# One weight quarter's load, issued on ScalarE's queue instead of SyncE's: a mixed linear and local attention block

## The chip, the cores and the metric

The kernel runs on one core of a Trainium2 chip. The metric is device time in microseconds (us): the median of several executions. All times inside an execution are counted from its first instruction, as the profile counts them.

## The reference

Two attention blocks of 2,048 tokens and width 1,024 read the same `x`. One is linear attention, the other local and dilated. A sigmoid gate mixes their outputs.

```python
x = A_x
g = _sigmoid((x * gate_w).sum(-1, keepdims=True))
a = _A_ref(x, A_wqkv, A_wo)      # linear attention: phi(q), phi(k), kv = sum of phi(k) v^T
b = _B_ref(x, B_wqkv, B_wo)      # 8 keys at distance 2, softmax
return g * a + (1 - g) * b
```

Only the first step matters here: `phi(k)` of block A, the projection `x @ wqkv[:, D:2D]`.

## The kernel before

The first thing that TensorE computes is the projection of the first four row blocks of `x` (128 rows each) on the key weights `WkA`. The weights come in two column halves of 512 columns, and each half in four k quarters of 256 rows (256 KB). The transposed `x` (called `xT`) comes in k quarters too: the first is loaded as plain rows and transposed on TensorE, the others by a transposing DMA.

```python
def load_rows(eng, t0, t1, d0=0, d1=D): ...     # x's rows, plain                     (L89)
def load_xT(k, t0, t1): ...                     # nc.sync.dma_start_transpose          (L95)
def load_wk(eng, k, h): ...                     # k quarter k of column half h, 256 KB (L99)
# ... (the identity for the transposes is made on VectorE)
with tc.manual_schedule(engines={SP, mybir.EngineType.Activation}):
    for kt in range(2):
        nc.scalar.dma_start(out=WkA[0][:, kt, :], in_=A_wqkv[kt * P:(kt + 1) * P, D:D + 512])
    load_rows(nc.sync, 0, 2, 0, 2 * P)
    load_rows(nc.sync, 2, 4, 0, 2 * P)
    load_wk(nc.sync, 0, 1)        # "the quarter": the one that the change moves
    load_xT(1, 0, 4)              # "xT's second quarter"
    load_wk(nc.sync, 1, 0)        # "the second load"
    load_wk(nc.sync, 1, 1)
    # ... k quarters 2 and 3, then everything else
```

TensorE works in program order:

```python
warm_up(26)                       # 26 small matmuls on ones
transpose_rows(0)                 # needs rows 0 and 1
for t in range(2): project(first[t], t, 0, 0)
transpose_rows(2)                 # needs rows 2 and 3
for t in range(2): project(first[t], t, 1, 0)
for half, ts in ((0, (2, 3)), (1, range(4))):   # half 1 needs the quarter: 9th projection matmul
    for kt in range(2):
        for t in ts: project(first[4 * half + t], t, kt, half)
for k in range(1, 4):             # k = 1 needs xT's second quarter and the second load: 17th
    for half in range(2):
        for t in range(4):
            for kt in (2 * k, 2 * k + 1): project(first[4 * half + t], t, kt, half)
    # ... phi on ScalarE and VectorE
```

Three landmarks are used below. **T** is the start of TensorE's first transpose (it needs rows 0 and 1). **H** is the start of the 9th projection matmul (it needs the quarter). **K** is the start of the 17th (it needs xT's second quarter and the second load).

The softmax here doesn't subtract the row's maximum and nothing guards it: scores larger than these inputs give would overflow.

## Time and profile before

| | before |
|---|---|
| time, three runs at first | 472.21 us median (472.11 to 472.75) |
| span of the profiled run | 470.1 us |
| TensorE busy | 466.1 us |
| T, H, K in the first profile | 3.74, 6.67, 8.46 us |
| matmuls from K to the last one of the kernel | last starts at 467.12 us |

TensorE is the bound, so the question is never how busy something else is, but where TensorE stands still. The prediction shows the lines for that. In all lines of the profile, PE is TensorE's matmuls and PEld its weight loads (which run ahead of the matmuls), DVE is VectorE, ACT ScalarE, POOL GpSimd; SPq is SyncE issuing DMAs; L196 is the line of the kernel with the projection matmul, L210 and L211 those of the transposes and their copies, L99 and L95 those of the loads.

### The profile page before, as it was taken

How to read it: one execution, taken by the hardware profiler on the slowest of the kernel's cores; microseconds unless marked ns; L12 is line 12 of the kernel's file. 1: busy time of each engine (PE TensorE's matmuls, PEld its weight loads, DVE VectorE, ACT ScalarE, POOL GpSimd, SP SyncE). 2: the span in 40 equal slices, each digit the busy share in tenths (PEclk: the TensorE clock that was granted, in tenths of full speed). 3: DMA queues.
4: the chain of work that ended last, by engine and by line, in shares of the span. 5: the costliest groups of instructions: out<-in, count | busy, mean ns of one | idle time of the engine just before them, and what ended most of it. 6: DMA issues, size and time to landing. Idle time of an engine off the chain costs nothing.

```text
span 470.1 us, 13202 instructions
## 1 busy us (share of the span) xinstructions
PE 466.1 (99%) x5762; PEld 268.8 (57%) x5762; DVE 278.4 (59%) x612; ACT 169.4 (36%) x277; POOL 15.7 (3%) x30
## 2 busy tenths in 40 slices
PE   8999999999999999999999999999999999999997
PEld 5444444445444444444888888888874444444444
DVE  2586689990219999999666676667660049800000
ACT  1343311112433333334455555555543234221121
POOL 1500000400000000000000000000000000000000
PEclk9999999999999999999999999999999999999999
DMA  9999970000644243627326525442463913211111
GB/s 222 206 218 374 348 244 0 0 1 1 216 134 123 83 141 123 157 97 244 111 55 108 112 52 87 104 93 62 83 172 67 234 57 79 73 52 45 34 33 46
DMA packets 98189, 55.14 MB, mean 117 GB/s; under 512 B 69075, under 2 KB 90579, under 8 KB 98131
## 3 DMA queue, kind: packets, MB, share of 16 engines
q1 hardware_dynamic: 93090, 49.87, 41.0%
q10 hardware_dynamic: 5040, 4.43, 2.9%
q8 instruction: 45, 0.74, 0.7%
q14 instruction: 14, 0.11, 0.1%
HBM read 26.10 MB, written 15.86 MB: 89 GB/s over the span
## 4 chain that ended last, share of the span: by engine, by line
PE 98%; DMA 1%; SPq 0%; DVE 0%; issue 0%; DVEq 0%
PE q_ps L421 26%; PE d_ps L627 12%; PE p_ps L325 12%; PE g_ps L264 12%; PE e_ps L627 12%; PE pk_ps L196 11%; PE p_ps L361 9%; PE po L501 2%; PE s2b L479 2%; DMA WkA<-in_A_wqkv_dram 1%; PE kv_ps L284 0%; PE w_ps L180 0%; SPq L89 0%; DVE osb L634 0%; DVEq L634 0%
## 5 line engine op out<-in xcount | busy, mean ns | idle before, releaser
L421 PE MATMUL q_ps<-xT,WqB 64*64 64x512 bf16 x1024 | 70.3, 376 | 0.0
L421 PE MATMUL q_ps<-xT,WkB 64*64 64x512 bf16 x1024 | 69.8, 376 | 0.0
L171 DVE TENSOR_SCALAR e<-e 128x512 f32<-128x512 f32 x64 | 27.3, 427 | 61.8 <-ACT e L170 61.8
L325 PE MATMUL p_ps<-WvB,xT 128*128 128x512 bf16 x256 | 57.4, 379 | 0.0
L196 PE MATMUL pk_ps<-WkA,xT 128*128 128x512 bf16 x256 | 55.8, 379 | 0.4 <-DVE xT L211 0.3
L264 PE MATMUL g_ps<-pk,xrow 128*128 128x512 bf16 x256 | 55.4, 379 | 0.0
L484 ACT ACTIVATE PT<-s2b 128x928 bf16<-128x928 f32 (+4 forms) x40 | 34.2, 855 | 49.8 <-PE s2b L479 48.8
L486 DVE TENSOR_TENSOR PT<-PT,mask 128x928 bf16<-128x928 bf16 (+4 forms) x40 | 23.6, 590 | 36.3 <-ACT PT L484 36.3
L421 PEld LDWEIGHTS <-WkB 64*64 64x64 bf16 x1024 | 40.4, 107 | 6.9 <-DMA vd<-tmp 0.2
L361 PE MATMUL p_ps<-WqA,xT 128*128 128x512 bf16 x192 | 43.4, 379 | 0.0
L627 PEld LDWEIGHTS <-pqT 128*128 128x128 bf16 x272 | 26.0, 98 | 29.6 <-issue 0.2
L627 PEld LDWEIGHTS <-OBT 128*128 128x128 bf16 x272 | 26.0, 98 | 29.4
L421 PEld LDWEIGHTS <-WqB 64*64 64x64 bf16 x1024 | 39.4, 107 | 5.6 <-DVE qz L461 0.2
L264 PEld LDWEIGHTS <-xrow 128*128 128x128 bf16 x256 | 25.0, 98 | 30.2
L196 PEld LDWEIGHTS <-xT 128*128 128x128 bf16 x256 | 24.8, 98 | 30.7 <-DVE xT L211 0.8
L325 PEld LDWEIGHTS <-xT 128*128 128x128 bf16 x256 | 24.9, 98 | 30.2 <-issue 0.5
L634 DVE TENSOR_SCALAR osb<-e_ps,omg 128x128 bf16<-128x128 f32 x1 | 0.4, 351 | 57.6 <-PE e_ps L627 57.6
L501 PEld LDWEIGHTS <-PT 64*56 64x56 bf16 (+2 forms) x1152 | 29.9, 104 | 4.5
L330 ACT CAST tmp<-p_ps 128x512 bf16<-128x512 f32 x32 | 18.7, 587 | 37.7 <-PE p_ps L325 32.8
L170 ACT ACTIVATE e<-pk_ps 128x512 f32<-128x512 f32 x32 | 18.9, 597 | 36.5 <-PE pk_ps L196 32.8
L361 PEld LDWEIGHTS <-xT 128*128 128x128 bf16 x192 | 18.8, 98 | 22.6
L627 PE MATMUL d_ps<-WoA,pqT 128*128 128x512 bf16 (+1 forms) x136 | 30.9, 370 | 0.0
(71 smaller groups left out, 544.3 us busy)
## 6 DMA issues: line engine op xcount, KB each, us to landing
vd<-tmp SPq DMA_DIRECT2D x16, 264.0 KB
out_dram<-osb ACTq DMA_DIRECT2D x31, 128.0 KB
xrow<-in_A_x_dram SPq DMA_DIRECT2D x3, 1024.0 KB
pqd<-tmp SPq DMA_DIRECT2D x12, 256.0 KB
WvA<-in_A_wqkv_dram SPq DMA_DIRECT2D x2, 1024.0 KB
WoA<-in_A_wo_dram SPq DMA_DIRECT2D x2, 1024.0 KB
WvB<-in_B_wqkv_dram SPq DMA_DIRECT2D x2, 1024.0 KB
WqA<-in_A_wqkv_dram SPq DMA_DIRECT2D x2, 1024.0 KB
```

The lines of the kernel that those rows point to most:

```text
L170: nc.scalar.activation(out=e[:], in_=pj[:], func=ACT.Exp)
L171: nc.vector.tensor_scalar(out=e[:], in0=e[:], scalar1=1.0, scalar2=1e-6, op0=ALU.min, op1=ALU.add)
L196: nc.tensor.matmul(pj[:], lhsT=xT[:, kt, t * P:(t + 1) * P], rhs=WkA[half][:, kt, :], start=(kt == 0), stop=(kt == KT - 1))
L264: nc.tensor.matmul(pj[:], lhsT=xrow[:, t, kt * P:(kt + 1) * P], rhs=pk[:, t, half * 512:(half + 1) * 512], start=(t == 0), stop=(t == NB - 1))
L325: nc.tensor.matmul(st["pj"][:], lhsT=xT[:, kt, t * P:(t + 1) * P], rhs=WvB[half][:, kt, :], start=(kt == 0), stop=(kt == KT - 1))
L330: nc.scalar.copy(out=v[:, half * 16:(half + 1) * 16, 0:Dh], in_=st["pj"][:].rearrange("p (h e) -> p h e", h=16))
L361: nc.tensor.matmul(st["pj"][:], lhsT=xT[:, kt, t * P:(t + 1) * P], rhs=WqA[half][:, kt, :], start=(kt == 0), stop=(kt == KT - 1))
L421: nc.tensor.matmul(banks[o][64 * j:64 * j + 64, :], lhsT=lhsT(r, kt, j), rhs=rhs(r, kt), start=first and kt == 0, stop=kt == KT - 1, skip_ ...
L484: nc.scalar.activation(out=pt[:, :, 0:W_], in_=s2b[:].rearrange("p a b s -> p (a b) s")[:, :, 0:W_], func=ACT.Exp, scale=SCALE)
L486: nc.vector.tensor_tensor(out=pt[:, :, 0:W_], in0=pt[:, :, 0:W_], in1=mask[:, None, base:base + W_].broadcast_to([P, 4, W_]), op=ALU.mult)
L501: nc.tensor.matmul(o2[64 * h:64 * h + w, par, s_, i, :], lhsT=pt[r, i, o:o + w], rhs=V[r, m, 4 * c + i, :], start=True, stop=True)
L627: nc.tensor.matmul(st["ps"][:, 0:n], lhsT=lhsT, rhs=W[c0 // 512][:, c, c0 % 512:c0 % 512 + n], start=(side == 0 and c == 0), stop=(side == ...
```

## The change

The quarter is needed by the 9th projection matmul, and TensorE waited for it. The change issues it on ScalarE's queue, behind the two loads that stand there. SyncE then has one issue less before xT's second quarter and the second load.

```diff
         for kt in range(2):
             nc.scalar.dma_start(out=WkA[0][:, kt, :], in_=A_wqkv[kt * P:(kt + 1) * P, D:D + 512])
+        load_wk(nc.scalar, 0, 1)
         load_rows(nc.sync, 0, 2, 0, 2 * P)
         load_rows(nc.sync, 2, 4, 0, 2 * P)
-        load_wk(nc.sync, 0, 1)
         load_xT(1, 0, 4)
         load_wk(nc.sync, 1, 0)
         load_wk(nc.sync, 1, 1)
```

## The prediction

> **What bounds the kernel now.** I read the page first, then who waited for whom on TensorE's two rows, then the chain that ended last over the first 12 us, then SyncE's issues, the bandwidth by stretch, and at last single instruction starts and the DMAs' semaphore increments in the trace. From the page of the kernel before, busy time and the chain:
>
> ```profile
> span 470.1 us, 13202 instructions
> ...
> PE 466.1 (99%) x5762; PEld 268.8 (57%) x5762; DVE 278.4 (59%) x612; ACT 169.4 (36%) x277; POOL 15.7 (3%) x30
> ...
> PE 98%; DMA 1%; SPq 0%; DVE 0%; issue 0%; DVEq 0%
> ```
>
> TensorE is busy for 466.1 of 470.1 us and is 98% of the chain that ended last. A load can only matter where TensorE waits for it. The view of waits of the weight-load row, from 3 to 12 us:
>
> ```profile
> PEld L196 <- DVE xT L211: 0.8, 2, 0.4
> PEld L196 <- DMA WkA<-in_A_wqkv_dram: 0.6, 1, 0.6
> PEld L210 <- DMA xrow<-in_A_x_dram: 0.2, 1, 0.2
> PEld L196 <- issue: 0.2, 1, 0.2
> ```
>
> The second line is the wait that the change is aimed at: WkA's second column half, first quarter (256 KB), which L120 issues. The 0.6 us is idle time of the weight loads, which run ahead of the matmuls, so it overstates what TensorE lost. The chain in order of time, same stretch:
>
> ```profile
> 1.82 4.79 DMA WkA<-in_A_wqkv_dram
> 6.62 0.05 issue
> 6.67 5.41 PE pk_ps L196 x24
> ```
>
> The DMA was issued at 1.82 and landed at 6.62 (1.82 + 4.79, rounded). From 6.67 the chain shows only projection matmuls. SyncE's issues, by the timeline of its queue, and the stretches (PE, PEld, DVE, ACT, POOL busy, clock, DMA share, GB/s):
>
> ```profile
> 0.80 0.98 SPq L89 DMA_DIRECT2D xrow<-in_A_x_dram  x2
> 1.82 0.47 SPq L99 DMA_DIRECT2D WkA<-in_A_wqkv_dram  x1
> 2.34 1.49 SPq L95 DMA_TRANSPOSE xT<-in_A_x_dram  x1
> 3.88 1.08 SPq L99 DMA_DIRECT2D WkA<-in_A_wqkv_dram  x2
> ```
>
> ```profile
> 4.50:6.75 2.25, 2.13 (x13) 0.84 (x13) 0.29 (x1) 0.41 (x2) 0.00 (x0) 1.00 1.03 163
> 6.75:8.50 1.75, 1.75 (x9) 0.75 (x10) 0.00 (x0) 0.00 (x0) 0.00 (x0) 1.00 1.12 324
> ```
>
> Taking the quarter off SyncE brings every later issue of SyncE forward by one slot, 2.34 - 1.82 = 0.52 us. But the DMA engines are full in both stretches (share 1.03 and 1.12), and in the first, in which the quarter and the transposed load of xT's second quarter are in flight together, they move only half the rate (163 against 324 GB/s).
>
> **How much TensorE really loses.** In the trace single 128x512 matmuls start 0.216 us apart when nothing holds them (6.665, 6.890, 7.106). The last matmul of the first column half's first quarter starts at 6.169, so the next could start at 6.385. It starts at 6.665: 0.28 us lost to the DMA. Eight matmuls follow. The last starts at 8.185 and the next could start at 8.401. It starts at 8.461: 0.06 us lost. From there to 115 us I find no gap of over 0.05 us between matmul starts, so everything behind 8.461 is rigid and moves as one piece.
>
> That second, small gap is the important one. The matmul at 8.461 is the first of the second k quarter, and waits for WkA's first column half, second quarter (issued at 3.88). The 16th and last semaphore increment of that DMA is at 8.42. The x rows for it (xT's second quarter) were there at 7.67. So **two loads stand in a row**: the one aimed at (landed 6.62) and the next one (landed 8.42), and only 0.04 us lie between the second landing and the rigid part. All the gain there can be is the two gaps, 0.28 + 0.06 = 0.34 us, or 0.07% of 472 us, and only if both loads land earlier. If the first alone does, TensorE runs its eight matmuls earlier and waits at the second.
>
> **What the Trainium skill says.** (1) "DMA: Bandwidth & Descriptors", section "Issuing engines are not separate DMA queues": transfers of all issuers run on the same 16 engines and interleave, and issuing from several saves only sequencer time. The trace agrees: ScalarE's two loads (queue q10) and the first rows (q1) are in flight side by side from 2.0 to 4.0 us. (2) Same page, "Queues, rings and completion order": each DMA engine takes turns between the queues that have work, packet by packet. So on ScalarE's queue the quarter no longer goes ahead of xT's transposed load, it shares with it, and it shares with the rows instead of coming behind them. No run shows yet what this sharing costs. (3) Same page, "Why a DMA increments its semaphore by 16 and not by 1": only all 16 mean that the data is there. Here that counts: the quarter's increments begin at 4.99 and four are in by 5.10, yet the other twelve come between 6.48 and 6.62. (4) "TensorE: Matmul & The Clock Gate", section "Wait — 56ns, not 53.3ns?", gives 215.7 ns between warm matmuls of 512 columns. The trace's 0.216 us agrees.
>
> **The change part by part.** Removed: one issue of 0.47 us from SyncE at 1.82. Added: one issue on ScalarE, whose two loads there (411 and 450 ns) end at 1.72; the third then ends near 2.2 (estimate from those), and ScalarE's first own work, the copy at 4.17, is not touched. Moved: the transposed load is issued at 1.82, the second quarter's first half near 3.36. Instructions and bytes are the same: nothing on TensorE, VectorE or in evictions changes, so the sum outside the first 8.5 us is zero.
>
> The quarter itself: 256 packets of 1 KB, 16 on an engine, about 46 ns each undisturbed, so 0.74 us of engine time. Its packets now start behind ScalarE's second load (landed 4.17), and not behind rows 2 to 3 (landed 4.51). On the face of it that is 0.3 us earlier, enough for the first gap of 0.28. But it then alternates with the transposed load, which was behind it in the ring.
>
> The second load: up to its landing the same five pieces have to pass: rows 256 KB, ScalarE's 256 KB, the quarter 256 KB, xT 256 KB, itself 256 KB, together 1,280 KB from 1.75 to 8.42 us, 197 GB/s. Engines that are full do not end sooner for another order of the same packets. Its landing moves only as far as the slow stretch gets shorter, somewhere from 0 to the 0.52 us of the earlier issue. I take some 0.15 us, which leaves 0.15 of the possible 0.34.
>
> **The rivals.** (a) *The whole gain*: if the slow stretch comes from descriptors that SyncE makes late (its transposed issues take 1.28 to 1.90 us each), both loads land up to 0.52 us earlier, and the full 0.34 us comes out: 471.9 us. Against it speaks the DMA share of 1.03 in that stretch. (b) *The next wait takes its place*: the quarter lands early, the second load stays at 8.42, and the matmul at 8.461 does not move: 472.2 us. For it speaks that all bytes ahead are the same. (c) *Contention makes it worse*: rows 2 and 3 landed at 4.51 and are used at 4.635, 0.12 us of slack. With the quarter's 16 packets among them they may be up to 0.74 us later, shifting TensorE by 0.62 us there: 6.385 + 0.62 = 7.0, plus eight matmuls of 0.216 is 8.73, against 8.461 a loss of 0.27 us. Likewise if the mixing slows the quarter to 7.1 us: 7.1 + 1.73 = 8.83, a loss of 0.37. That makes 472.5 to 472.6 us. For it speaks that the mixed stretch is the slow one already. (d) *Something later*: an earlier SyncE queue could upset the loads behind. They have room: xT's fifth row block lands at 14.97 and its first use, 48 matmuls after 8.461, is near 18.8.
>
> **Range and chances.** I hold (a) for a quarter, (b) or between (a) and (b) for a half, (c) for a quarter. 0.25 x -0.34 + 0.5 x -0.1 + 0.25 x 0.3 is about -0.06, and leaning a little to the intent I say -0.1: 472.1 us. The spread of the runs is larger than the effect: three runs before were 472.11, 472.21 and 472.75, and the profiled one 471.84. Low end: 471.84 less 0.34 is 471.5, rounded out to 471.4. High end: 472.75 plus half of the loss of (c) is 472.9. A difference of 2% is 9.4 us, some 28 times all the waiting that the change can reach, so within 2% is all but certain: 0.98, with 0.01 on either side for what I don't see.
>
> **What would show it.** Right: the DMA wait of 0.6 us is shorter or gone; the first matmul of the second k quarter starts between 8.1 and 8.5; the wait in front of it has grown; and TensorE has no new gap behind. Wrong: that matmul starts after 8.5 (contention), with the first rows or the quarter landing late; or before 8.1, which would need a shorter path than TensorE's own; or any change in instruction counts, clock or the stages behind 10 us.

## The result

The changed kernel takes 472.06 us (median of six runs, 471.83 to 472.46), the kernel before 472.16 us in the six runs it was compared with (471.75 to 472.75). The ratio is 0.9998, with a 95% interval from 0.9985 to 1.0011: the same. Ratios here are the mean time of one kernel's runs over that of the other's of the same rounds, so not quite the ratio of the quoted medians.

The page of the changed kernel has the same instructions and the same shape:

```profile
PE 466.2 (99%) x5762; PEld 265.9 (57%) x5762; DVE 278.1 (59%) x612; ACT 169.6 (36%) x277; POOL 15.7 (3%) x30
...
PE 99%; DMA 1%; DVE 0%; issue 0%; DVEq 0%
```

The waits of TensorE's weight loads from 3 to 12 us, all of them (what waited, for what, us in total, times, longest):

```profile
PEld L196 <- DVE xT L211: 0.8, 2, 0.4
PEld L210 <- DMA xrow<-in_A_x_dram: 0.4, 1, 0.4
```

The wait for WkA's load is gone, as intended. The wait for x's first rows is 0.2 us longer. The chain that ended last, in order of time over the first 12 us (start, us, what; pieces left out at the dots):

```profile
0.80 3.01 DMA xrow<-in_A_x_dram
...
4.60 0.60 PE pk_ps L196 x2
5.20 0.22 PE xt_ps L210 x4
5.43 6.71 PE pk_ps L196 x31
```

No load stands in the chain behind x's first rows. SyncE's queue, by the timeline (start, us, engine line, operation):

```profile
1.83 1.34 SPq L95 DMA_TRANSPOSE xT<-in_A_x_dram  x1
3.23 1.09 SPq L99 DMA_DIRECT2D WkA<-in_A_wqkv_dram  x2
```

The transposing load is issued at 1.83 and not at 2.34, the second load at 3.23 and not at 3.88. The DMA engines' rate by stretch (columns as in the prediction; the last two are the DMA share and GB/s):

```profile
4.50:6.75 2.25, 2.15 (x13) 1.04 (x14) 0.33 (x2) 0.60 (x2) 0.00 (x0) 1.00 1.17 235
6.75:8.50 1.75, 1.75 (x9) 0.78 (x8) 0.00 (x0) 0.00 (x0) 0.00 (x0) 1.00 1.13 303
```

The slow stretch moved 235 GB/s, where it had moved 163. (This did not last: over four profiles each it is 127 to 174 before and 163 to 235 after.) From the semaphore increments in the trace, the quarter landed at 6.29 (6.62 before) and the second load at 8.02 (8.42 before). K came at 8.30 us and not at 8.46: **0.16 us earlier**, in spite of a T that was 0.12 us later (3.86 against 3.74).

So where did 0.16 us go, with spans of 470.12 us before and 470.15 after? Comparing the starts of the same matmuls in both traces, the changed kernel is 0.16 us ahead from K up to 333.7 us. There TensorE starts no matmul for 0.17 us (333.748 to 333.917, in the middle of the small attention matmuls), and from there on it is 0.03 us behind. Nothing that the profile shows as a wait belongs to it.

On these two profiles one would say: the change works, gains 0.16 us at the start, and an accident ate it. The experiments show that this reading is wrong in its first half.

### The profile page after: what moved, and what is told of

Its sections match the earlier page's. It is cut to its first block, busy times and chain, and to the rows that moved or that the text cites. A ratio compares the mean times of both kernels' runs of the same rounds, so it can differ in the third digit from the quotient of the medians.

```text
span 470.1 us, 13202 instructions
## 1 busy us (share of the span) xinstructions
PE 466.2 (99%) x5762; PEld 265.9 (57%) x5762; DVE 278.1 (59%) x612; ACT 169.6 (36%) x277; POOL 15.7 (3%) x30
## 3 DMA queue, kind: packets, MB, share of 16 engines
q10 hardware_dynamic: 5312, 4.69, 3.1%
## 4 chain that ended last, share of the span: by engine, by line
PE 99%; DMA 1%; DVE 0%; issue 0%; DVEq 0%
PE q_ps L421 26%; PE d_ps L627 12%; PE p_ps L325 12%; PE pk_ps L196 12%; PE g_ps L264 12%; PE e_ps L627 12%; PE p_ps L361 9%; PE po L501 2%; PE s2b L479 2%; DMA xrow<-in_A_x_dram 1%; PE kv_ps L284 0%; PE w_ps L180 0%; PE xt_ps L210 0%; DVE osb L634 0%; DVE xT L211 0%
```

## The experiments

Twelve runs were made, in three calls of four; the record names another chip for each call (8, 0 and 14), and times are compared within a call. Each run gave a profile, and one or five times. The theory at the start: the order of the loads sets K, and the change gains by the freed issue slot or by the second queue. The rivals: the landings scatter from run to run by as much as they differ; or TensorE's own pace sets K.

This table has all fourteen profiles. C is the time at which TensorE's clock opens: matmuls of 512 columns start 0.43 us apart before it and 0.216 us after it. Where the trace has a record of the clock, C is from that record, else (marked ~) from the spacing. Landings are the last of a DMA's 16 semaphore increments. "us" is the time of the profiled execution. In all traces but the two first, the record of the last matmul before K is missing (the weight loads are complete), so a gap of 0.43 us there is not a wait.

| run | us | T | C | quarter landed | xT's 2nd quarter | second load | K | us - K | what K followed |
|---|---|---|---|---|---|---|---|---|---|
| before, 1st | 471.84 | 3.74 | 3.77 | 6.62 | 7.67 | 8.42 | 8.46 | 463.4 | second load |
| before_again | 471.79 | 3.75 | 3.81 | 6.46 | 7.48 | 8.37 | 8.41 | 463.4 | second load |
| before_r3 | 472.07 | 3.67 | 5.53 | 6.63 | 7.67 | 8.42 | 8.66 | 463.4 | TensorE |
| before_r4 | 471.73 | 3.85 | ~4.6 | 6.44 | 7.50 | 8.26 | 8.34 | 463.4 | TensorE |
| after, 1st | 471.88 | 3.86 | 4.04 | 6.29 | 7.31 | 8.02 | 8.30 | 463.6 | TensorE |
| after_again | 471.79 | 3.65 | ~4.9 | 6.63 | 7.63 | 8.35 | 8.41 | 463.4 | quarter |
| after_r3 | 471.73 | 3.69 | 3.54 | 6.57 | 7.61 | 8.32 | 8.36 | 463.4 | quarter |
| after_r4 | 472.36 | 3.72 | 6.14 | 6.82 | 7.87 | 8.57 | 8.97 | 463.4 | TensorE |
| slot | 472.78 | 3.63 | 6.56 | 6.81 | 7.76 | 8.48 | 9.13 | 463.6 | TensorE |
| same_queue | 472.19 | 3.70 | 5.80 | 6.84 | 6.12 | 7.74 | 8.79 | 463.4 | TensorE |
| second_late | 472.65 | 3.65 | 6.81 | 6.51 | 7.54 | 8.95 | 9.27 | 463.4 | TensorE |
| no_quarter | 472.04 | 3.67 | ~4.9 | none | 6.17 | 6.99 | 8.36 | 463.7 | TensorE |
| plain_first | 473.31 | 3.71 | 5.50 | 7.46 | 9.84 | 8.13 | 9.89 | 463.4 | xT's 2nd quarter |
| rows_split | 473.46 | 3.57 | 4.39 | 8.19 | 6.05 | 8.46 | 9.97 | 463.5 | quarter |

The column "us - K" is the reason why K is the right thing to look at: the time of an execution is K plus 463.4 us, in eleven of fourteen within 0.1, and in the other three with one small slip of TensorE behind K (0.15 to 0.25 us), like that at 333.7 us.

### before_again and after_again: the same two kernels once more

No edit; five rounds each.

> The kernel before, once more, for the spread of the landmarks that the argument uses. Landmarks are matmul starts: T (first transpose of x's rows, 3.735 us in the first profile), H (9th projection matmul, the first that needs the quarter that was moved; 6.665), K (17th, the first that needs the second k quarter; 8.461). If the two waits are a property of the order of the loads, H is again held by the DMA (6.5 to 6.8) and K starts again within 0.1 us of the second load's landing (8.3 to 8.6). If they were an accident of one run, H comes near 6.38 and K near 8.11. Ratio of the times 1.000 either way, within 0.001.

Measured: ratio 1.0002 (0.9988 to 1.0015), for two identical kernels. H started at 6.51 and K at 8.41, 0.04 us behind the second load's landing. The chain shows that load:

```profile
4.13 4.23 DMA WkA<-in_A_wqkv_dram
8.37 0.04 issue
8.41 3.61 PE pk_ps L196 x16
```

The prediction's claim that the second load stands right behind the quarter, and holds K, holds in two profiles.

> The changed kernel, once more. In its first profile T was 3.858, H 6.575, K 8.302 and no wait for a load stood between T and the end of the projection. Theory: the change takes both waits away, so that K follows from T alone: K - T = 4.44 us again, within 0.03. If the 0.12 us later T is contention of the moved quarter with x's first rows, T is again 3.8 to 3.9; if it is the run-to-run spread of a landing, T falls somewhere from 3.7 to 3.9. The late slip of 0.19 us that TensorE showed near 333.8 us should not come back at the same place if it is not the change's doing. Time: 0.9997 of before if K is 0.16 us earlier and nothing is given back, which five rounds will hardly tell from 1.000.

Measured: 472.18 us against 472.42, ratio 0.9997 (0.9985 to 1.001). Two expectations failed. The quarter landed at 6.63, later than in either profile of the kernel before, and was waited for (the view of waits as above):

```profile
PEld L196 <- DMA WkA<-in_A_wqkv_dram: 0.4, 1, 0.4
PEld L210 <- DMA xrow<-in_A_x_dram: 0.3, 1, 0.3
```

And K - T was 4.76 us, not 4.44. K is 8.41, as in before_again to the hundredth. T was 3.65, so the late T of the first profile is more likely scatter than contention (without the change T was as late as 3.85, in before_r4). The slip at 333.7 us did not come back.

### slot: is it the freed issue slot?

```diff
+        nc.sync.dma_start(out=pk[:, NB - 2, 0:16], in_=A_wqkv[0:P, 0:16])   # 4 KB, overwritten later
         load_xT(1, 0, 4)
```

(base: the changed kernel)

> The changed kernel with a tiny load (32 bytes per partition, 4 KB in all) put where the quarter's issue used to stand on SyncE, so that the transposed load and the second load are issued as late as before (about 2.3 and 3.9 us), while the quarter stays on ScalarE's queue. Theory A (the gain comes from the freed issue slot): the second load lands near 8.4 again and K goes back to 8.4 to 8.5. Theory B (the gain comes from two queues feeding the DMA engines side by side, which keeps them fuller from 4.5 to 6.75 us): the second load lands by 8.2, and K follows from T alone, K - T = 4.44. In both the quarter lands before 6.5 and H is not held by it.

Measured: the second load was issued at 3.83 and landed at 8.48, which is theory A's number. But the quarter landed at 6.81, which neither theory had, and K was 9.13, far behind any load. The matmuls tell why: they start 0.43 us apart up to 6.5 us. TensorE's clock opened only at 6.56 us. This was the first sign of what the table's column C shows. For the question that it was made for, the run is inconclusive.

### same_queue: is it the order or the second queue?

```diff
-        load_wk(nc.sync, 0, 1)
         load_xT(1, 0, 4)
+        load_wk(nc.sync, 0, 1)
         load_wk(nc.sync, 1, 0)
```

(base: the kernel before)

> The kernel before with the quarter and the transposed load of xT's second quarter swapped on SyncE's queue: the transposed load is then issued as early as in the changed kernel (1.83 us), but the quarter comes behind it in the same ring. If order and bytes are all, the quarter lands behind 256 KB of transposed rows, at 7.0 to 7.7 us, H is held until then, and K = H + 8 x 0.216 is at 8.8 to 9.5, a loss of 0.3 to 1.0 us. If the second queue was not needed for the gain (the transposed load only had to be issued earlier), the quarter lands by 6.4 and H and K are as in the changed kernel.

Measured: the quarter landed at 6.84, only 0.2 to 0.4 us later than in the kernel before, though 256 KB more stood in front of it. The second load was issued at 3.82, as late as in the kernel before (3.88), and landed at 7.74, which is 0.28 us or more earlier than in any profile of the changed kernel, which issues it at 3.23. So, as far as one profile shows, the issue time of the second load doesn't by itself set its landing, and theory A's number in the run before was no proof of theory A. The rate in the slow stretch:

```profile
4.50:6.75 2.25, 2.25 (x11) 1.16 (x12) 0.29 (x1) 0.59 (x2) 0.00 (x0) 1.00 1.01 264
```

264 GB/s, with one queue for all of it. K was 8.79 and followed TensorE's clock (C 5.80), not a load.

### plain_first: why is the stretch slow?

```diff
         load_wk(nc.sync, 0, 1)
-        load_xT(1, 0, 4)
         load_wk(nc.sync, 1, 0)
         load_wk(nc.sync, 1, 1)
+        load_xT(1, 0, 4)
```

(base: the kernel before)

> The kernel before (quarter on SyncE) with the transposed load of xT's second quarter put behind both plain loads of the second k quarter. It tests why the DMA engines move only 150 to 235 GB/s from 4.5 to 6.75 us. Theory M (a transposed load in flight together with plain loads slows both): the quarter lands by 5.5, the second load by 6.5, at 300 GB/s or more, and the transposed load last, by 8.0; no load is waited for and K is TensorE's own, 8.1 to 8.2 with an early clock. Theory S (the first loads of a kernel are slow whatever they are): the quarter lands at 6.3 or later, the transposed load after 8.4, and K is held by it. Times: 0.9995 to 1.000 of before, not to be told apart by five rounds.

Measured: 472.45 us against 472.12, ratio 1.0009 (0.9995 to 1.0022). Theory M is wrong: with the transposing load out of the way the quarter landed at 7.46, later than ever. Theory S foretold the landings, and that K is held by the transposing load:

```profile
PEld L196 <- DMA xT<-in_A_x_dram: 1.0, 1, 1.0
PEld L196 <- DMA WkA<-in_A_wqkv_dram: 0.9, 1, 0.9
```

But "the first loads are slow" is not the reason either. The slow stretch moved to where the transposing load now stands, long after the first loads:

```profile
4.50:6.75 2.25, 2.25 (x12) 0.99 (x12) 0.29 (x1) 0.60 (x2) 0.00 (x0) 1.00 0.88 238
6.75:8.50 1.75, 1.35 (x7) 0.50 (x6) 0.00 (x0) 0.00 (x0) 0.00 (x0) 1.00 1.21 133
```

133 GB/s at a DMA share of 1.21. The single DMA packets in the trace show what happens. A transposing load's packet of 256 bytes takes 18 ns as a rule. Some take more than 350 ns, and these end together:

```
                 packets over 350 ns   the first   they end     last plain packet ahead
                 of the transposing    of them     (us)         of it ends (us)
                 load                  starts
before, 1st      13                    4.96        6.39-6.42    6.19
before_again     15                    4.89        6.22-6.26    6.03
before_r3        18                    4.86        6.39-6.43    6.20
before_r4        19                    4.92        6.24-6.28    6.04
plain_first      19                    6.59        8.68-8.71    8.47
```

In all five, these packets stay open until the last plain packet that stood ahead of the transposing load has ended; the first of them ends 0.19 to 0.21 us after it. From 7.75 to 8.5 us of plain_first some five plain packets of 46 ns run in each quarter of a microsecond: that is one DMA engine at its full pace (0.25 / 0.046), while some 19 transposed packets stand open, counted as busy. The reading that fits: **a transposing load stops part-way until the last DMA engine has reached it, and the engines wait there for each other.** It is inferred from these times, as the trace does not name the engine of a packet; with up to 19 packets on 16 engines, some engine must have two open. Nor does the whole load wait: 393 to 485 of its 1,024 packets had ended before the last plain packet did. The slow stretch is largely this waiting. Its length is the lag of the last engine, 1.3 to 2.1 us here. In the changed kernel, with the quarter on the other queue, the same hold-up is shorter (the longest transposed packet took 0.56 to 1.18 us in its four profiles, 1.34 to 1.55 in the four of the kernel before), but the quarter and the second load did not land earlier for it on average, as the last experiment shows. Where the lag comes from is less clear: single plain packets of the quarter took far longer than 46 ns between 3.8 and 5.6 us, the longest 0.54 to 1.53 us in each of the eight profiles of the two kernels. What held those packets stays open.

### second_late: is the second load really next in line?

```diff
-        load_wk(nc.sync, 1, 0)
         load_wk(nc.sync, 1, 1)
+        load_wk(nc.sync, 1, 0)
```

(base: the changed kernel)

> The changed kernel with the two halves of the second k quarter swapped on SyncE's queue, so that the one that TensorE needs first (the second load) is issued and lands one place later. It landed at 8.02 and 8.35 us in the two profiles of the changed kernel, with the other half 0.7 us behind. Theory (the second load stands next in line and sets K, the start of the 17th projection matmul): it lands at 8.7 to 9.1 and K starts within 0.1 us of that, 0.3 to 0.8 us later than in the changed kernel, and a wait for it appears. Rival (K follows from TensorE's own pace and clock, loads have room): K stays at 8.3 to 8.5. If TensorE's clock opens late in this run (after 5.5 us), K is late for that reason and the wait is shorter; the matmul spacing tells.

Measured: the second load landed at 8.95, inside the expected range, but K came only at 9.27, and no wait for it appears. C was 6.81, the latest of all, so this is the escape clause of the expectation. Inconclusive for the question; for TensorE's own pace it is the outermost point.

### no_quarter: the ceiling

```diff
-        load_wk(nc.scalar, 0, 1)
...
-        rhs=WkA[half][:, kt, :]
+        rhs=WkA[half if kt > 1 else 0][:, kt, :]
```

(shown against the changed kernel; wrong in half of the keys of block A, though the comparison with the reference still passed its tolerance)

> The ceiling: the changed kernel without the moved quarter. The first quarter of the second column half is computed with the first half's weights, so half of the result is wrong on purpose. No wait for the quarter can exist and 256 KB fewer go before the second load. If the loads' bytes set the start, the second load lands 0.7 us or more earlier (7.3 to 7.6), no load is waited for after the first rows, and K is TensorE's own: with the clock open by 4.0 us K is at 8.1 to 8.2, 0.25 to 0.35 us before the kernel before's; with the clock opening at 6.5 us K is at 9.1 to 9.4 all the same. First rows: if the moved quarter delays them, T is under 3.7 here; T has been 3.74, 3.75 before and 3.86, 3.65 after.

Measured: the second load landed at 6.99, earlier than expected, and no load but x's first rows is waited for:

```profile
PEld L195 <- DVE xT L210: 0.8, 2, 0.4
PEld L209 <- issue: 0.3, 1, 0.3
PEld L209 <- DMA xrow<-in_A_x_dram: 0.2, 1, 0.2
```

K was 8.36, TensorE's own pace with the clock opening near 4.9 us. Even with the quarter gone for good, this execution took 472.04 us, of which 0.25 us is a slip behind K.

### rows_split: can x's first rows come earlier?

```diff
+        load_rows(nc.scalar, 1, 2, 0, 2 * P)
         for kt in range(2): ...
-        load_rows(nc.sync, 0, 2, 0, 2 * P)
+        load_rows(nc.sync, 0, 1, 0, 2 * P)
```

(base: the changed kernel)

> The changed kernel with x's first two row blocks loaded 64 KB each by SyncE and ScalarE at once, ahead of the weights, instead of 128 KB by SyncE beside ScalarE's weights. TensorE's last warm-up matmul starts at 3.456 and its first transpose T waited until 3.65 to 3.86 for these rows. If the rows share the DMA engines with the weights, both pieces land by 3.4 and T comes at 3.5 to 3.6, 0.1 to 0.3 us earlier; the first weights then land near 3.9 instead of 3.4, still before the first projection matmul (4.4). If the rows' landing is latency and not sharing, T stays at 3.6 to 3.9. K follows T only where no load and no late clock stands between.

Measured: the rows landed at 2.98 and 3.15, and T came at 3.57, the earliest of all, as expected. What was not expected: the quarter, now fourth on ScalarE's queue, was issued only at 3.00 (0.79 us after the third issue there had ended; why is open), and landed at 8.19. The view of waits:

```profile
PEld L197 <- DMA WkA<-in_A_wqkv_dram: 1.9, 1, 1.9
```

The chain of the same run:

```profile
3.00 5.19 DMA WkA<-in_A_wqkv_dram
8.19 0.05 issue
8.24 1.68 PE pk_ps L197 x7
```

The 0.1 us at T was lost fifteen times over at H. In this execution the version is worse: the quarter has too little room before its need to be issued 1.2 us later.

### before_r3, before_r4, after_r3, after_r4: the loads or the clock?

By now there was a new theory: C scatters over some 3 us from run to run, whatever the kernel, and the loads matter only where C is early. No edit in these four.

> The kernel before, third profile, to test a theory that came out of the first ten profiles: that what TensorE does at the start is set by when its clock opens, and by the loads only where it opens early. C is the time from which 512-column matmuls start 0.216 us apart and not 0.427 us; it was 3.77 and 3.81 in the two profiles of the kernel before, and anywhere from 4.04 to 6.81 in the others. K is the start of the 17th projection matmul. Theory (clock): C differs from run to run of one and the same kernel; with C under 4.6, K is held by the second load at 8.37 to 8.50 and the waits for the quarter stand; with C over 5, the waits for the loads shrink or vanish in this kernel too, and K is 8.11 + 0.38 x (C - 3.77), within 0.15, by the end points 8.11 (worked out for C 3.77) and 9.27 (C 6.81). Rival (the change sets it): C is 3.7 to 3.9 again, since the kernel before always had it so, and K is 8.4 to 8.5.

> The kernel before, fourth profile, for the same test as the third: by the clock theory C lies anywhere between 3.7 and 7.1 us, and K is the later of 8.4 to 8.5 (loads) and 8.11 + 0.38 x (C - 3.77) (TensorE's own pace). By the rival C is 3.7 to 3.9 and K 8.4 to 8.5. The time of the profiled run should follow K: 471.8 at K 8.4, 472.6 at K 9.2, within 0.3.

> The changed kernel, third profile and five more rounds. By the clock theory C lies anywhere between 3.7 and 7.1 us, and K is 8.11 + 0.38 x (C - 3.77) within 0.15, the same law as for the kernel before, only without its floor of 8.4 to 8.5 where the quarter lands by 6.4. By the rival (the change makes C late: 4.04 and about 4.9 in its two profiles) C is again over 4.0 here and in the fourth. Timed: on average the gain can only come from runs with C under 4.6, about a quarter of them, with 0.1 to 0.3 us each: 0.05 us, a ratio of 0.9999; the rounds will say the same within 0.001.

> The changed kernel, fourth profile, for the same test. The quarter landed at 6.29 and 6.63 here, at 6.62 and 6.46 in the kernel before. If the change lands it earlier as such, it is under 6.4 in at least one of the third and fourth profile and over 6.4 in both of the kernel before; if the spread of landings is as large as the change, the four of both kernels overlap.

Measured: C was 5.53 and about 4.6 in the kernel before, 3.54 and 6.14 in the changed one. The rival, by which the change makes C late, is out: both kernels have early and late ones. In before_r3, with C at 5.53, the *unchanged* kernel shows no wait for any weight load:

```profile
PEld L196 <- DVE xT L211: 0.8, 2, 0.4
PEld L210 <- issue: 0.6, 2, 0.3
PEld L210 <- DMA xrow<-in_A_x_dram: 0.2, 1, 0.2
```

The quarter landed at 6.63 there, as late as in the first profile, but TensorE came for it only after that. Its chain shows the slow clock: two projection matmuls and four transposes take 1.04 and 0.31 us, where the changed kernel's first profile has 0.60 and 0.22 in the same places:

```profile
4.45 1.04 PE pk_ps L196 x2
5.48 0.31 PE xt_ps L210 x4
5.79 2.82 PE pk_ps L196 x13
```

And in after_r3, with C at 3.54, the *changed* kernel waits for the quarter as long as the kernel before did (the view of waits, then the chain):

```profile
PEld L196 <- DMA WkA<-in_A_wqkv_dram: 0.6, 1, 0.6
```

```profile
3.23 5.08 DMA WkA<-in_A_wqkv_dram
8.32 0.04 issue
8.36 3.83 PE pk_ps L196 x17
```

The chain names the second load, as it landed 0.04 us before K. But TensorE hardly waited for it: from H to K are 1.741 us here, against 1.737 in after_again, where the quarter alone held TensorE. It is the quarter that set K.

K by the rough law 8.11 + 0.38 x (C - 3.77) should have been 8.78 in before_r3 and 9.01 in after_r4; it was 8.66 and 8.97, within the 0.15 that was allowed. In before_r4 it was 8.34, below the expected floor of 8.4, because the second load landed at 8.26. The landings of the quarter overlap: 6.44 to 6.63 (mean 6.54) in four profiles of the kernel before, 6.29 to 6.82 (mean 6.58) in four of the changed one. So do those of the second load: 8.26 to 8.42 (mean 8.37) and 8.02 to 8.57 (mean 8.32). The five rounds of after_r3 gave a ratio of 0.9998 (0.9984 to 1.0011).

## Why the prediction was right, and where its steps were not

The time, 472.06 us for a predicted 472.1, the range, and "within 2%" were right, and the reason for the last was right too: everything that the change can reach is 0.34 us of waiting, against 9.4 us for 2%. That the two medians differ by 0.10 us, as predicted, is luck: the interval of the ratio spans -0.7 to +0.5 us. The three comparisons of the changed kernel gave 0.9998, 0.9997 and 0.9998. Each by itself can't be told from 1, and the comparison of the kernel before with itself was at 1.0002. If there is a gain, it is too small for these runs. K, which has less scatter, shows none: its mean over four profiles is 8.47 before and 8.51 after.

- **TensorE is the bound, and what lies behind K is rigid**: right. From the first matmul of the next stage to the kernel's last it is 406.86 us in all four profiles of the kernel before, and 406.87 in three of the changed one. The exception, 407.05, is the slip at 333.7 us; slot and no_quarter have one as well. The prediction had no such slips.
- **Two waits, 0.28 and 0.06 us**: right for the profile it was read from, and too much as a property of the kernel. In the second profile they were 0.11 and 0.16 us. In the third and fourth no matmul was late for a weight's DMA (before_r4 shows 0.2 us of it on the weight-load row alone). An estimate of the most that earlier landings of the weights could give, from these four: K without any wait would have been 8.11 (the prediction's 6.385 + 8 x 0.216), 8.13 (worked out the same way), 8.66 and 8.34, a mean of 8.31 against the measured mean of 8.47. So 0.16 us on average, and not 0.34.
- **The second load stands right behind the quarter and takes over the wait**: half right. In before and before_again K waited for it, and starts 0.04 us after its landing. But rival (b) and the sign "the wait in front of it has grown" asked for that wait in the changed kernel, and there it grew in none of four profiles: K followed TensorE's own pace or the quarter. What took the gain away was not the next load but that the quarter itself, on average, did not land earlier (below).
- **The issue slot**: right in itself, 1.83 for 2.34 and 3.23 for 3.88 us. (Beside it, ScalarE's copy at 4.17 is not its first own work: a table load runs from 0.80 to 2.08 us. Nothing rests on that.)
- **"On the face of it that is 0.3 us earlier, enough for the first gap"**: this step failed. The first profile agreed (6.29), the mean of four did not (6.58 against 6.54).
- **"I take some 0.15 us"** for the second load's landing: mis-sized. Means of 8.37 and 8.32 make it 0.05 us, inside the scatter of 0.16 us before and 0.55 us after. The size of K in the first profile, 0.16 us earlier, agreed with the prediction by luck.
- **"Engines that are full do not end sooner for another order of the same packets"**: this step failed. A share of 1.03 is not a full engine. In the four profiles of the kernel before, 31 to 53% of the packets' time from 4.5 to 6.75 us belongs to transposed packets that were open for over 350 ns, and another order (same_queue, one profile) landed the second load 0.5 to 0.7 us earlier than in the kernel before.
- **Rival (c), contention with rows 2 and 3**: they landed at 4.37 to 4.56 (mean 4.47) before and at 4.41 to 4.94 (mean 4.69) after, so 0.22 us later on average. Whether that comes from the quarter is open: they landed at 4.43 in no_quarter, which speaks for it, but at 4.97 in same_queue, where the quarter stood behind them on SyncE. It cost little: where it was latest (after_r4) the clock was slow as well. That profile also shows the prediction's sign for (c), K after 8.5 with the rows and the quarter late, and yet no matmul waited for either: the sign could not tell contention from a late clock.
- **The rival that was missing: TensorE's clock.** The prediction took 0.216 us between matmuls from one profile as given from T on. In fact C falls anywhere from 3.54 to 6.81 us in fourteen profiles, and K with it from 8.30 to 9.27 where no load is late. That is 1 us, three times the waiting at stake. With a late clock TensorE comes so late for the quarter that its landing doesn't matter. This also fits the scatter of the timed executions of one kernel (471.61 to 473.40 us before): in the profiled ones the time is K + 463.4. It does not cover all of it: 473.40 would need a K of 10.0, and a late clock gave 9.27 at most. That each slow timed execution had a late clock was not seen, as those have no trace.

Why C scatters: the Trainium skill, "TensorE: Matmul & The Clock Gate", section "What's actually happening", says that the clock is opened by a monitor that looks at a window of 3,413 ns which runs freely and doesn't start with the kernel. The fourteen values of C span 3.27 us with the same TensorE work up to 3.46 us in all of them, which agrees with a start at any phase of such a window. The traces also have a grid of that length: in all eleven that record the clock, the full clock lasted 467.626 or 464.213 us, which is 137 or 136 times 3.4133 us, whether it began at 3.54 or at 6.81. No run here changes the phase, so that the phase is the cause is read from the page and not shown.

Left open: whether the change gains 0.1 us on average, or nothing, or loses a little; what delays single packets of the quarter by up to 1.5 us, and TensorE's rare slips of 0.15 to 0.25 us.

## What to carry to other kernels

When a change aims at a wait of a few tenths of a microsecond at the start of a kernel, take several profiles of the kernel *before* first: here one profile showed waits that two of the next three didn't have. Find the landmark that the time follows (here K, with time = K + 463.4 us), and compare it and the landings over runs, because the time alone can't resolve them. And don't read a DMA share of 1 as bandwidth used up: look at GB/s beside it, and at whether packets of a transposing load stand open meanwhile.

## What the Trainium skill lacked or had wrong

- "TensorE: Matmul & The Clock Gate", section "What's actually happening", puts the scatter of the clock's opening at about ±500 ns. Here it was 3.54 to 6.81 us over fourteen profiles. The same section's window of 3.4 us fits that and the recorded lengths of the full clock (136 and 137 windows), its ±500 ns doesn't.
- The same section asks for a busy window of about 3.4 us before the clock opens. In after_r3 it opened at 3.54 us, 2.70 us after the first matmul (0.84).
- No page has it: the clock column of a stretch reads 1.00, and the mean granted clock of the execution 0.999, also where matmuls start at half pace (before_r3, 4.4 to 5.3 us, spacing 0.40 to 0.43 us). The spacing of the matmuls shows it, those numbers don't.
- "DMA: Bandwidth & Descriptors", section "DMA Transpose (X-bar)", doesn't say that a transposing load can stop behind plain loads, with the DMA engines waiting for each other (inferred here). Its packets stayed open for up to 2.11 us and ended together, from 0.19 to 0.21 us after the last plain packet ahead of the load on; meanwhile the core moved 127 to 174 GB/s at a DMA share over 1 (kernel before, 4.5 to 6.75 us).
- The same page gives no scatter for the landings of one and the same load. The same 256 KB load in the same kernel landed at 6.29 to 6.82 us from run to run.
